# An attention and routing kernel on one core: a table-driven order of instructions in which small table pieces move behind a later GpSimd subtraction, and the first pair of heads runs in another order

## The chip, the cores and the metric

The kernel runs on one core of a Trainium2 chip. Five engines work side by side, each on its own list of instructions: PE (TensorE, matrix products), DVE (VectorE), ACT (ScalarE), POOL (GpSimd) and SP (SyncE, which here only issues transfers). An engine takes its list strictly in order; if the next instruction waits for another engine, everything behind it waits too. The metric is the time of one execution on the device, in microseconds (us). The kernel before was timed at 1265.13 us (median of 3 runs, 1263.82 to 1270.05). Its profile comes from one separate execution.

## What is computed

Attention over 64 heads with queries averaged in pairs of rows, then a mixture of experts with a greedy, capacity-limited assignment of tokens. Cut to what matters:

```python
# q, k, v: 8 x 8 x 1152 x 64 (q and k 8 times as wide as v)
q_pool = q.reshape(8, 8, 576, 2, 64).mean(axis=3)
scores = q_pool @ k.transpose(0, 1, 3, 2) / 8
scores = scores - scores.max(-1)
attn = exp(scores) / sum(exp(scores))
x = (attn @ v).transpose(0, 2, 1, 3).reshape(4608, 512)
logits = x @ w_gate                        # 4608 tokens x 8 experts
for idx in argsort(-logits.flatten()):     # greedy: best pair first,
    tok, e = idx // 8, idx % 8             # at most 576 tokens an expert
    if assigned[tok] < 0 and counts[e] < 576:
        assigned[tok] = e; counts[e] += 1
for e in range(8):
    out[assigned == e] = relu(x[assigned == e] @ w1[e]) @ w2[e]
```

## The kernel before, in words

The 64 heads are taken as 32 pairs. A pair needs 18 steps (two heads, nine blocks of 128 keys each). In a step (`step`, L734) PE forms scores of 128 keys against 576 queries (`sc`, L751), ACT takes their exponential into `P` (L754), and a remainder `PM` = `P` minus its leading half is formed by one subtraction of 128 x 576 elements (L758), on POOL in 16 of the 18 steps of a middle pair and on DVE in the other two. PE then uses `P` and `PM` as weights in the weighted sum of the values (`av`, L768).

Beside the steps of one pair the next pair is prepared. Queries and keys are split into a leading half and a remainder: `QH` and `KH` by ACT (L583, L601), `QL` and two halves of `KL` by DVE from two inputs (L591, L610). SP's transfers bring these into the layouts `QA`, `QB`, `KA`, `KB` and `BD`. The raw queries `QS` arrive by a transfer of SP, and POOL's queue issues a second one that adds the odd rows (L486). A bound on the scores of each query is needed: PE multiplies leading halves (`ma`, `mb`, L668), DVE takes maxima of them into `MX` (L671, L680), folds them into `CM` (L703), PE transposes it and DVE writes the bound row `AU` (L724), which goes into `QB`. Scores of the next pair can't start without it. Before the split, `bounds` finds the scales `SC` and the exponent's factor `EX` from sums of absolute values that ACT takes (L507).

The first pair differs. Its maxima run a head at a time (`max_chunk`, L649 to L662), in 15 pieces of 384 columns a head, for which the first head may use the banks of `sc` and `av` too, since nothing else uses them yet. Its remainders `QL` and `KL` and those of the second pair come from POOL.

Small constant tables for the routing (`routing_tables`) are made while attention runs: POOL makes index rows first, and then `pieces`, each one or two small instructions (`before` L326, `upto` L327, `e8`, `pcol`, four of `nib` with L331, `diag` L335 to L337, `slots` L340, `jval` L342, and two more), one a pair from the early pairs on. One piece, `same16` (L338, L339), is on DVE.

The order of instructions is written by a table of numbers. Every operation has a tag, a running number and the pair that it belongs to; its due time is the tag's number from `TAU` plus 25 for each pair (`TAU0`, `TAU1` and `TAU2` hold the first three pairs). `Cycle.plan` emits, among the operations whose inputs have been emitted, always the one with the lowest due time. So the tables alone say in which order each engine's list stands. The pieces have the tag `tab`, the piece on DVE `tad`. Operations of the second pair get their times of adding from `at` (L906).

Of the kernel before, what the change touches and what calls it, by code (L numbers as in the profile page):

```python
# [152 lines left out]
class Cycle(Order):  # L153
# [11 lines left out]
    def plan(self):  # L165
# [27 lines left out]
TAU = {"abs": [-48.4833, -47.0605, -38.3773], "aug": [-21.4881], "augd": [-11.2262, 4.4303], "augt": [-4.3451],  # L193
# [3 lines left out]
       -301.8994, -63.224, -198.6406, -15.9845, -78.5836, 33.7202, -197.7787], "bdd": [-52.3637, -285.2947], "best":  # L197
       [30], "el": [-77.0706], "ex": [-50.7557], "expa": [-16.6599, -154.184, -20.8529, 5.9927, 12.6026, 14.7889,
       -14.7359, -29.1238, -104.9479], "expb": [-32.523, -130.2187, -27.9823, 14.3985, 17.5253, -281.0359, 9.6164,
# [3 lines left out]
       [-70.8466, -187.4708], "ldq": [-65.2457], "ldv": [-277.9826], "ldw": [2.8], "me": [-19.8978, -10.7115,  # L203
# [6 lines left out]
       [2.7664, 4.9823, 6.5534, 8.0795, 9.6086, -181.5656, 16.9348, 19.0221, 21.216], "qkb": [5.2308, 7.0644, 8.3738,  # L210
       12.1143, 0.0557, 20.0132, 22.5039, 25.3261, 28.3165], "ql": [-38.1313], "rc": [9.2364, -9.47], "sc":
       [-36.4174], "scv": [-30.065], "spr": [-21.9235, -31.1405, -21.9627, -26.5265, -22.5479, -164.2155, -315.3032,
       -74.6622, -15.1485, -17.1123, -19.956, -16.4269], "store": [-95.7261], "sx": [16.3692, 22.2312, 0.8466,
       -61.2066, -78.1894], "tab": [-69.9737], "tad": [-127.8336], "tap": [-44.6145, -41.1498, -47.4908, -31.2065],
       "vh": [-26.7285, -47.8828], "vl": [-23.1603, -21.3115], "vs": [-148.6017, -208.4574], "vsh": [-168.3274],
       "wsq": [12.8365], "x": [-94.3595, -7.6786]}
TAU0 = {"abk": [-60.377, -62.9993], "abs": [-96.8953, -53.0217], "aug": [-7.39949, -0.804], "augt": [-7.399491,
# [5 lines left out]
        -7.026297, 1.533201, 4.734301, 9.325501, 23.883701], "expb": [-7.399487, -7.399467, -7.399445, -7.399424,  # L223
        1.198702, 3.416501, 5.503401, 22.1687, 22.168703], "fill": [-10.2794, -126.6764, -30.3842, -147.957,
        -245.9624, -174.4366, -139.2362, -212.3909, -147.5215, -160.7165, -141.2792, -181.6421], "fold": [-7.399497,
# [11 lines left out]
        1.5332, 4.7343, 9.3255, 23.8837], "qkb": [-7.399488, -7.399468, -7.399446, -7.399425, 1.198701, 3.4165,  # L237
        5.5034, 13.319, 22.168702], "ql": [-29.9917], "qs": [-147.1978], "rc": [9.181703, 25.133714], "sc":
        [-60.376997], "scv": [-37.467499], "spr": [-60.376977, -38.883998, -35.21, -60.37698, -31.0808, -29.991699,
# [6 lines left out]
TAU1 = {"abs": [-34.9327, -39.4214, -46.3877], "aug": [-1.025495], "augd": [-1.025494, -1.025493], "augt":  # L246
# [29 lines left out]
def routing_tables(nc, pool, ident, jp, scratch, do):  # L276
# [14 lines left out]
    it = {}  # L291
# [59 lines left out]
def attention(ctx, tc, top, kt, qt, v, wg, w1, x_dram, L, npair=NPAIR):  # L351
# [297 lines left out]
    def max_chunk(n, j, c, z, t):  # L649

        i = n % 2
        if n == 0:
            h, j = j // 5, j % 5
            banks = [(ma, "ma"), (mb, "mb")]
            if not h:
                banks += [(sc[a // 2][:, a % 2], ("sc", a // 2, a % 2)) for a in range(4)] + [(av[b], f"av{b}") for b in range(2)]
            m, mk = banks[z % len(banks)]
# [993 lines left out]
```

## Time and profile before

| | |
|---|---|
| timed runs, median of 3 | 1265.13 us (1263.82 to 1270.05) |
| the profiled execution, its time | 1275.09 us |
| its span, first to last instruction | 1273.3 us |
| PE busy | 1202.7 us, 94% |
| DVE busy | 1034.3 us, 81% |
| ACT busy | 974.6 us, 77% |
| POOL busy | 905.9 us, 71% |
| mean granted TensorE clock | 0.98 |

The span is what the profile's rows cover; the time of the profiled execution is 1.8 us more. Attention with everything beside it takes about the first 800 us, routing and the experts the rest. The busy shares are means over the whole span: which engine holds up which is read from the rows of a stretch.

### The profile page before, as it was taken

To read this page: it belongs to the slowest core of one execution; us is meant where nothing else is said; L and a number is where in the kernel's file an instruction comes from. 1 tells how busy PE (TensorE), PEld (TensorE's weight loads), DVE (VectorE), ACT (ScalarE), POOL (GpSimd) and SP (SyncE) were. 2 spreads that over 40 slices of the span, in tenths; PEclk is the share of its full clock that TensorE was granted. 3 is DMA by queue.
4 is the path that set the end of the run, shared out by engine and by line. 5 is a ranking of instruction groups with operands and counts; after the bars stand their busy time and mean duration, and the time that the engine had idled before them with its cause. 6 is when DMAs were issued, how large, how long until landed. Compare 5 with 4: busy or idle time off the path is not lost.

```text
span 1273.3 us, 38899 instructions
## 1 busy us (share of the span) xinstructions
PE 1202.7 (94%) x15470; PEld 865.0 (68%) x15470; DVE 1034.3 (81%) x2743; ACT 974.6 (77%) x1719; POOL 905.9 (71%) x879
## 2 busy tenths in 40 slices
PE   7899899898999999999999999789899899999998
PEld 2567677776777777877777778565657466565563
DVE  5889899898999999999999995788878788884520
ACT  6779789797899999999999986076765676767751
POOL 5779799697889988888898897055756474665641
PEclk7999999898999999999999999999999999999999
DMA  6676677566667768677776731043254454537401
GB/s 184 159 187 171 155 174 189 142 163 164 170 162 196 178 163 203 169 171 192 174 187 162 183 91 37 20 170 112 97 195 125 133 172 135 170 124 230 119 30 38
DMA packets 131218, 190.83 MB, mean 150 GB/s; under 512 B 50268, under 2 KB 86108, under 8 KB 128732
## 3 DMA queue, kind: packets, MB, share of 16 engines
q1 hardware_dynamic: 117948, 126.75, 37.9%
q0 software_dynamic: 12944, 61.58, 17.0%
q8 instruction: 121, 1.98, 0.7%
q14 instruction: 61, 0.50, 0.1%
q10 hardware_dynamic: 144, 0.02, 0.0%
HBM read 116.41 MB, written 18.87 MB: 106 GB/s over the span
## 4 chain that ended last, share of the span: by engine, by line
PE 69%; DVE 17%; ACT 4%; issue 3%; DMA 3%; SPq 1%; POOL 1%; another core or an unknown queue 1%; POOLq 0%; ACTq 0%; DVEq 0%
PE sc L751 19%; PE av L768 16%; PE ph L1536 9%; PE po L1566 8%; PE mb L668 5%; PE ma L668 4%; DVE MX L671 2%; DVE KL L610 1%; PE av L803 1%; DMA XG<-XB 1%; DVE PM L758 1%; DVE GE L1163 1%; DVE HX L1545 1%; DMA BD<-QH 1%; PE av L815 1%
## 5 line engine op out<-in xcount | busy, mean ns | idle before, releaser
L758 POOL TENSOR_TENSOR PM<-P 128x576 f16<-128x576 f32 x508 | 618.3, 1277 | 117.2 <-ACT P L754 65.2
L754 ACT ACTIVATE P<-sc,EX 128x576 f32<-128x576 f32 x576 | 412.7, 738 | 97.2 <-PE sc L751 84.2
L768 PEld LDWEIGHTS <-P 128*128 128x128 bf16 x5760 | 297.2, 98 | 31.3 <-issue 2.6
L768 PE MATMUL av<-V,P 128*128 128x65 f16 (+1 forms) x5760 | 305.3, 193 | 0.0
L768 PE MATMUL av<-V,PM 128*128 128x65 f16 x2880 | 296.4, 195 | 0.0
L768 PEld LDWEIGHTS <-PM 128*128 128x128 f16 x2880 | 265.7, 97 | 0.0
L751 PE MATMUL sc<-QA,KA 128*128 128x288 f16 x1152 | 236.7, 287 | 1.6 <-ACT P L754 1.3
L751 PE MATMUL sc<-QB,KB 65*128 65x288 f16 (+1 forms) x1152 | 237.9, 287 | 0.0
L671 DVE TENSOR_REDUCE MX<-mb 128x1 f32<-128x512 f32 x279 | 190.9, 684 | 32.3 <-PE mb L668 27.3
L671 DVE TENSOR_REDUCE MX<-ma 128x1 f32<-128x512 f32 x279 | 191.0, 685 | 13.3 <-PE ma L668 10.1
L751 PEld LDWEIGHTS <-KA 128*128 128x128 f16 x1152 | 106.9, 97 | 86.0 <-issue 34.9
L1566 PE MATMUL po<-W2H,HX 128*128 128x512 f16 x512 | 156.9, 381 | 0.3 <-ACT OT L1568 0.3
L1536 PE MATMUL ph<-XH,W1H 128*128 128x320 f16 (+1 forms) x512 | 146.3, 286 | 0.7 <-DVE WE L1514 0.3
L1536 PE MATMUL ph<-XL,W1H 128*128 128x320 f16 (+1 forms) x512 | 146.2, 286 | 0.8 <-DVE XL L1395 0.3
L1536 PE MATMUL ph<-XH,W1L 128*128 128x320 f16 (+1 forms) x512 | 145.9, 286 | 0.9 <-issue 0.9
L751 PEld LDWEIGHTS <-KB 65*128 65x128 f16 (+1 forms) x1152 | 113.3, 98 | 30.4
L1566 PEld LDWEIGHTS <-HX 128*128 128x128 f16 x768 | 71.6, 98 | 86.4 <-issue 9.6
L1588 POOL DMA_INDIRECT out_dram<-OT,idx x40 | 39.1, 979 | 118.9 <-ACT OT L1568 99.7
L668 PE MATMUL mb<-KH,BD 128*128 128x512 f16 x279 | 107.3, 384 | 13.6 <-DVE AU L724 11.3
L1536 PEld LDWEIGHTS <-W1H 128*128 128x128 f16 x1024 | 97.5, 98 | 33.2 <-issue 7.7
L668 PE MATMUL ma<-KH,BD 128*128 128x512 f16 x279 | 106.8, 383 | 5.9 <-DMA BD<-QH 2.4
L1489 POOL TENSOR_TENSOR W2L<-W,W2H 128x512 f16<-128x512 f32 x64 | 73.3, 1158 | 40.8 <-ACT W L1487 33.6
(308 smaller groups left out, 2169.7 us busy)
## 6 DMA issues: line engine op xcount, KB each, us to landing
KD<-in_kt_dram SPq DMA_DIRECT2D x64, 288.0 KB
VD<-in_v_dram SPq DMA_DIRECT2D x32, 576.0 KB
WB<-in_w_dram SPq DMA_DIRECT2D x32, 512.0 KB
QA<-QH SPq DMA_DIRECT2D x128, 72.0 KB
KA<-KH SPq DMA_DIRECT2D x64, 144.0 KB
KA<-KL SPq DMA_DIRECT2D x64, 144.0 KB
KB<-KH SPq DMA_DIRECT2D x64, 144.0 KB
x_dram<-X SPq DMA_DIRECT2D x16, 576.0 KB
```

The lines of the kernel that those rows point to most:

```text
L610: fn=lambda h=h: nc.vector.scalar_tensor_tensor(KL[n % 2][:, h], KD[n % 2][:, h], KS, KH[i][:, h], op0=OP.mult, op1=OP.subtract),
L668: od.add(t, "PE", 214, lambda: nc.tensor.matmul(m, BD[i][:, j, :], KH[i][:, 512 * c:512 * c + 512], start=True, stop=True), r=bd + [("KH", ...
L671: od.add(t, "DVE", 597, lambda: nc.vector.tensor_reduce(MX[i][:, j, c:c + 1], m, axis=AX.X, op=OP.max), r=[mk], w=[("MX", i, j, c)], tag=" ...
L751: nc.tensor.matmul(c[:, t, :288], a[i][:rows, s, ks], b[i][:rows, s, 288 * t:288 * t + 288], start=first, stop=not first)
L754: od.add(g + 0.1, "ACT", 624, lambda: nc.scalar.activation(p.rearrange("p (t q) -> p t q", t=2), c[:, :, :288], AF.Exp, scale=EX[n % 3][:, ...
L758: od.add(g + 0.2, en, dur, lock=1, fn=lambda: eng.tensor_tensor(pm, p, hi, op=OP.subtract), r=[("P32", g % NP)], w=[("PM", g % NM)], tag="pm")
L768: nc.tensor.matmul(out, w[:, qs], v, start=kb == 0 and j == 0 and y == 0, stop=kb == NKB - 1 and y == 2, skip_group_check=True)
L803: nc.tensor.transpose(m[:, 128 * z:128 * z + 128], X[u][:, 3 * q + z], ident)
L1489: od.add(tt, "POOL", 1230, lambda o=lo[p], a=raw[p], h=hi[p]: nc.gpsimd.tensor_tensor(o, a, h, op=OP.subtract), r=[key, hk, sk], w=[(nm + ...
L1536: nc.tensor.matmul(p, a[:, d, fs], b[:, d, qs], start=z == 0, stop=z == 11)
L1566: nc.tensor.matmul(o, a[:, z, q0:q0 + 128], b[:, z], start=z == 0 and y == 0, stop=z == 7 and y == 2)
L1588: st = nc.gpsimd.indirect_dma_start(out=out, out_offset=bass.IndirectOffsetOnAxis(ap=idx[i][:n, c:c + 1], axis=0), in_=OT[ob][:n], in_offs ...
```

## The change

It has two parts, and both alter orders and hardly any operations.

In the steady run, the due time of the tag `tab` goes from -69.97 to -60.4, and the DVE piece is cut into two pieces of one instruction each.

In the first pair and the beginning of the second, new numbers in `TAU0`, `TAU1` and `at` give: five banks instead of eight for the first head's maxima and two in turn for the second's; the first head's bound row directly behind its fold; the first exponentials ahead of ACT's sums of absolute values for the second pair; and one clearing of `KB` on POOL in another place. The numbers of `TAU2`, and those of `TAU` other than `tab`, are the same.

```diff
-       ... "tab": [-69.9737], ...
+       ... "tab": [-60.4], ...
...
-TAU1 = {"abs": [-34.9327, -39.4214, -46.3877], ...
+TAU1 = {"abs": [-32.3994884, -32.3994916, -46.3877], ...
...
-        (1000, lambda: (nc.vector.tensor_scalar(it["m"], it["m"], 15, None, op0=OP.bitwise_and),
-                       nc.vector.tensor_scalar(C["same16"], it["m"], 0.0, None, op0=OP.is_equal))),
+        (1000, lambda: nc.vector.tensor_scalar(it["m"], it["m"], 15, None, op0=OP.bitwise_and)),
+        (1000, lambda: nc.vector.tensor_scalar(C["same16"], it["m"], 0.0, None, op0=OP.is_equal)),
...
-            banks = [(ma, "ma"), (mb, "mb")]
-            if not h:
-                banks += [(sc[a // 2][:, a % 2], ("sc", a // 2, a % 2)) for a in range(4)] + [(av[b], f"av{b}") for b in range(2)]
-            m, mk = banks[z % len(banks)]
+            if h:
+                m, mk = ((ma, "ma"), (mb, "mb"))[z % 2]
+            else:
+                m, mk = ((ma, "ma"), (av[0], "av0"), (sc[0][:, 0], ("sc", 0, 0)), (av[1], "av1"), (sc[1][:, 0], ("sc", 1, 0)))[(5 * c + j) % 5]
...
-                at.update(load=-61.5, vload=-57, split=-42.5, bound=-42, spread=-34, val=-36, mm=-20, fold1=1, aug=1.5)
+                at.update(load=-61.5, vload=-57, split=-31.6, bound=-31.15, spread=-23.5, val=-29, mm=-20, fold1=1, aug=1.5)
```

The lists below show the orders that follow. A row names the line, the operation, and its tiles as out<-in with buffer numbers. Lines of the kernel after stand five higher (L758 is L763 there, L591 is L596, L327 is L332).

POOL's list around the piece `upto` and the transfer of `QS0` that follows it, before:

```order
L758 TENSOR_TENSOR PM3_153<-P323_143 128x576
L758 TENSOR_TENSOR PM6_156<-P326_146 128x576
L327 TENSOR_SCALAR upto_176<-jp_70 128x128
L758 TENSOR_TENSOR PM5_155<-P325_145 128x576
L758 TENSOR_TENSOR PM7_157<-P327_147 128x576
L758 TENSOR_TENSOR PM0_150<-P320_140 128x576
L758 TENSOR_TENSOR PM9_159<-P329_149 128x576
L758 TENSOR_TENSOR PM2_152<-P322_142 128x576
L758 TENSOR_TENSOR PM1_151<-P321_141 128x576
L758 TENSOR_TENSOR PM3_153<-P323_143 128x576
L486 DMA QS0_124<-in_qt_dram 128x576
```

And the same stretch of POOL's list after:

```order
L763 TENSOR_TENSOR PM3_153<-P323_143 128x576
L763 TENSOR_TENSOR PM6_156<-P326_146 128x576
L763 TENSOR_TENSOR PM5_155<-P325_145 128x576
L763 TENSOR_TENSOR PM7_157<-P327_147 128x576
L763 TENSOR_TENSOR PM0_150<-P320_140 128x576
L763 TENSOR_TENSOR PM9_159<-P329_149 128x576
L763 TENSOR_TENSOR PM2_152<-P322_142 128x576
L763 TENSOR_TENSOR PM1_151<-P321_141 128x576
L332 TENSOR_SCALAR upto_176<-jp_70 128x128
L763 TENSOR_TENSOR PM3_153<-P323_143 128x576
L491 DMA QS0_124<-in_qt_dram 128x576
```

The piece moved from the fourth place of the stretch to the place just ahead of the last subtraction before the transfer. The other pieces move to the same place, each between the same two transfers of `QS` as before.

DVE's list where the `same16` piece stands before, among the maxima of a pair (`MX1`):

```order
L671 TENSOR_REDUCE MX1_139<-mb_171 128x1
L338 TENSOR_SCALAR scratch_112<-scratch_112 128x128
L339 TENSOR_SCALAR same16_182<-scratch_112 128x128
L680 TENSOR_REDUCE MX1_139<-ma_170 128x4
L671 TENSOR_REDUCE MX1_139<-mb_171 128x1
L671 TENSOR_REDUCE MX1_139<-ma_170 128x1
L671 TENSOR_REDUCE MX1_139<-mb_171 128x1
```

And where it stands after, later in the same pair:

```order
L685 TENSOR_REDUCE MX1_139<-mb_171 128x4
L676 TENSOR_REDUCE MX1_139<-ma_170 128x1
L343 TENSOR_SCALAR scratch_112<-scratch_112 128x128
L344 TENSOR_SCALAR same16_182<-scratch_112 128x128
L596 SCALAR_TENSOR_TENSOR QL0_91<-QS0_124,SC2_115,QH0_89 128x576
L615 SCALAR_TENSOR_TENSOR KL0_87<-KD0_119,SC2_115,KH0_85 128x576
L763 TENSOR_TENSOR PM8_158<-P328_148 128x576
```

The two instructions moved from the middle of the pair's maxima to the place just ahead of `QL` and `KL`.

ACT's list around the first exponentials of the program (`P321`, `P320`, `P323`, `P322`), before:

```order
L507 ACTIVATE VJ_134,VQ_128<-VD1_123 128x1152
L507 ACTIVATE VJ_134,VM1_127<-QS1_125 128x576
L507 ACTIVATE VJ_134,VM1_127<-KD1_120 128x1152
L754 ACTIVATE P321_141<-sc1_167,EX0_116 128x576
L539 ACTIVATE SC1_114<-VE1_136 128x2
L547 ACTIVATE EX1_117<-SC1_114 128x1
L548 ACTIVATE EX1_117<-VE1_136 128x1
L583 ACTIVATE QH1_90<-QS1_125,SC1_114 128x576
L754 ACTIVATE P320_140<-sc0_166,EX0_116 128x576
L754 ACTIVATE P323_143<-sc1_167,EX0_116 128x576
L601 ACTIVATE KH1_86<-KD1_120,SC1_114 128x576
```

And after:

```order
L512 ACTIVATE VJ_134,VQ_128<-VD1_123 128x1152
L759 ACTIVATE P321_141<-sc1_167,EX0_116 128x576
L512 ACTIVATE VJ_134,VM1_127<-QS1_125 128x576
L759 ACTIVATE P320_140<-sc0_166,EX0_116 128x576
L512 ACTIVATE VJ_134,VM1_127<-KD1_120 128x1152
L759 ACTIVATE P323_143<-sc1_167,EX0_116 128x576
L544 ACTIVATE SC1_114<-VE1_136 128x2
L552 ACTIVATE EX1_117<-SC1_114 128x1
L553 ACTIVATE EX1_117<-VE1_136 128x1
L759 ACTIVATE P322_142<-sc0_166,EX0_116 128x576
L588 ACTIVATE QH1_90<-QS1_125,SC1_114 128x576
```

Three exponentials of the first head now stand ahead of or between the sums L507 (now L512), and `SC1`, `EX1` and `QH1` of the second pair stand behind them. SP's list is the same before and after, so its transfers that need `QH1` stay ahead of those that bring the second head's keys.

## Rows read from the trace of the kernel before

**Rows 1.** Stretches: window, length, PE, PEld, DVE, ACT, POOL busy (count), clock, DMA, GB/s.

```profile
120.00:330.00 210.00, 198.75 (x3203) 156.56 (x3202) 190.10 (x351) 177.17 (x308) 169.19 (x156) 0.96 0.64 160
440.00:780.00 340.00, 338.61 (x5659) 268.93 (x5656) 306.66 (x608) 305.36 (x525) 293.93 (x252) 1.00 0.67 165
```

**Rows 2.** Timeline at 126 us, DVE: start, us, engine, line, operation, tiles, count.

```profile
126.34 0.80 DVE L591 SCALAR_TENSOR_TENSOR QL<-QS,SC,QH 128x576 f16<-128x576 f32 x1
...
127.79 1.70 DVE L758 TENSOR_TENSOR PM<-P 128x576 f16<-128x576 f32 x1
130.43 3.29 DVE L610 SCALAR_TENSOR_TENSOR KL<-KD,SC,KH 128x576 f16<-128x576 f32 x1
```

**Rows 3.** Timeline at 126 us, ACT, POOL and PE; in brackets the idle time before.

```profile
126.24 1.36 ACT L754 ACTIVATE P<-sc,EX 128x576 f32<-128x576 f32 x2
...
127.73 1.15 POOL L758 TENSOR_TENSOR PM<-P 128x576 f16<-128x576 f32 x1 [1.51 <-issue]
...
129.47 3.62 POOL L758 TENSOR_TENSOR PM<-P 128x576 f16<-128x576 f32 x3
...
134.90 0.38 PE L668 MATMUL mb<-KH,BD 128*128 128x512 f16 x1 [3.35 <-DVE AU L724]
```

**Rows 4.** Timeline at 697 us, the same place of a later pair: DVE, ACT, POOL.

```profile
697.73 0.81 DVE L591 SCALAR_TENSOR_TENSOR QL<-QS,SC,QH 128x576 f16<-128x576 f32 x1
...
698.21 1.36 ACT L754 ACTIVATE P<-sc,EX 128x576 f32<-128x576 f32 x2
...
699.18 0.75 DVE L758 TENSOR_TENSOR PM<-P 128x576 f16<-128x576 f32 x1
...
699.70 1.24 POOL L758 TENSOR_TENSOR PM<-P 128x576 f16<-128x576 f32 x1 [2.09 <-issue]
```

**Rows 5.** Timeline at 223 and 422 us, the same place of two other pairs, and 302 us.

```profile
223.65 1.36 ACT L754 ACTIVATE P<-sc,EX 128x576 f32<-128x576 f32 x2
223.70 0.80 DVE L591 SCALAR_TENSOR_TENSOR QL<-QS,SC,QH 128x576 f16<-128x576 f32 x1
...
302.49 4.59 DVE L610 SCALAR_TENSOR_TENSOR KL<-KD,SC,KH 128x576 f16<-128x576 f32 x1 [0.25 <-issue]
...
422.15 1.36 ACT L754 ACTIVATE P<-sc,EX 128x576 f32<-128x576 f32 x2
422.16 0.80 DVE L591 SCALAR_TENSOR_TENSOR QL<-QS,SC,QH 128x576 f16<-128x576 f32 x1
```

**Rows 6.** Timeline, DVE's `QL` of four more pairs.

```profile
177.50 0.80 DVE L591 SCALAR_TENSOR_TENSOR QL<-QS,SC,QH 128x576 f16<-128x576 f32 x1
...
276.40 0.81 DVE L591 SCALAR_TENSOR_TENSOR QL<-QS,SC,QH 128x576 f16<-128x576 f32 x1
...
444.78 0.80 DVE L591 SCALAR_TENSOR_TENSOR QL<-QS,SC,QH 128x576 f16<-128x576 f32 x1
...
743.65 0.80 DVE L591 SCALAR_TENSOR_TENSOR QL<-QS,SC,QH 128x576 f16<-128x576 f32 x1
```

**Rows 7.** Timeline, POOL's table pieces `upto`, one of `nib`, and `diag`.

```profile
118.52 0.54 POOL L327 TENSOR_SCALAR upto<-jp 128x128 bf16<-128x128 int32 x1
...
216.03 0.25 POOL L331 TENSOR_SCALAR nib<-scratch 128x16 f32<-128x16 int32 x1
...
320.04 0.37 POOL L335 TENSOR_SCALAR scratch<-scratch 128x64 f32<-128x64 int32 x1
320.48 0.38 POOL L336 TENSOR_SCALAR diag<-scratch 128x64 f16<-128x64 int32 x1
```

**Rows 8.** Timeline at 343 us, PE behind the DVE pieces.

```profile
343.35 0.38 PE L668 MATMUL ma<-KH,BD 128*128 128x512 f16 x1 [1.08 <-DVE MX L680]
```

**Rows 9.** Timeline, first pair: ACT and SP's queue.

```profile
26.79 0.74 ACT L754 ACTIVATE P<-sc,EX 128x576 f32<-128x576 f32 x1 [3.32 <-PE sc L751]
28.04 0.76 ACT L583 ACTIVATE QH<-QS,SC 128x576 f16<-128x576 f32 x1
...
37.78 0.60 SPq L617 DMA_DIRECT2D KB<-KH  x1
```

More of the change, by code (lines that the diff above doesn't have):

```diff
@@ L192 @@
 PERIOD = 25.0
-TAU = {"abs": [-48.4833, -47.0605, -38.3773], "aug": [-21.4881], "augd": [-11.2262, 4.4303], "augt": [-4.3451],
[3 rows of a table removed]
-       -301.8994, -63.224, -198.6406, -15.9845, -78.5836, 33.7202, -197.7787], "bdd": [-52.3637, -285.2947], "best":
-       [30], "el": [-77.0706], "ex": [-50.7557], "expa": [-16.6599, -154.184, -20.8529, 5.9927, 12.6026, 14.7889,
-       -14.7359, -29.1238, -104.9479], "expb": [-32.523, -130.2187, -27.9823, 14.3985, 17.5253, -281.0359, 9.6164,
[3 rows of a table removed]
-       [-70.8466, -187.4708], "ldq": [-65.2457], "ldv": [-277.9826], "ldw": [2.8], "me": [-19.8978, -10.7115,
[6 rows of a table removed]
[L210 to L216, printed above, removed]
@@ L217 @@
-TAU0 = {"abk": [-60.377, -62.9993], "abs": [-96.8953, -53.0217], "aug": [-7.39949, -0.804], "augt": [-7.399491,
[5 rows of a table removed]
-        -7.026297, 1.533201, 4.734301, 9.325501, 23.883701], "expb": [-7.399487, -7.399467, -7.399445, -7.399424,
-        1.198702, 3.416501, 5.503401, 22.1687, 22.168703], "fill": [-10.2794, -126.6764, -30.3842, -147.957,
-        -245.9624, -174.4366, -139.2362, -212.3909, -147.5215, -160.7165, -141.2792, -181.6421], "fold": [-7.399497,
[11 rows of a table removed]
-        1.5332, 4.7343, 9.3255, 23.8837], "qkb": [-7.399488, -7.399468, -7.399446, -7.399425, 1.198701, 3.4165,
-        5.5034, 13.319, 22.168702], "ql": [-29.9917], "qs": [-147.1978], "rc": [9.181703, 25.133714], "sc":
-        [-60.376997], "scv": [-37.467499], "spr": [-60.376977, -38.883998, -35.21, -60.37698, -31.0808, -29.991699,
[6 rows of a table removed]
@@ L246 @@
-TAU1 = {"abs": [-34.9327, -39.4214, -46.3877], "aug": [-1.025495], "augd": [-1.025494, -1.025493], "augt":
[6 rows of a table removed]
-        -16.355199, -23.751799, -15.081299, -21.213299, -10.492399, -18.345799, -13.433399, -1.025498], "mre":
-        [-27.9644, -1.0255, -8.404399], "qa": [-68.5572], "qh": [-32.399481], "ql": [-28.143899], "sc": [-32.399483],
-        "scv": [-24.0828], "spr": [-32.39945, -9.0591, -32.399452, -32.399477, -17.2565, -9.3805, -32.399451, -1.8944,
-        -32.399453, -32.399478, -32.399476, -5.7004], "vd": [1.4358, 1.435801], "vh": [-24.082798, -24.082799], "vl":
-        [1.435803, 1.435802], "vs": [-32.399489, -32.399485], "vsh": [-32.399484]}
@@ L258 @@
-TAU2 = {"abs": [-44.485199, -38.0633, -27.5185], "aug": [-0.158697], "augd": [-0.158696, -0.158695], "augt":
[10 rows of a table removed]
+TAU = {"abs": [-48.4833, -47.0605, -38.3773], "aug": [-21.4881], "augd": [-11.2262, 4.4303], "augt":
[4 rows of a table added]
+       -197.7787], "bdd": [-52.3637, -285.2947], "best": [30], "el": [-77.0706], "ex": [-50.7557], "expa":
+       [-16.6599, -154.184, -20.8529, 5.9927, 12.6026, 14.7889, -14.7359, -29.1238, -104.9479], "expb":
+       [-32.523, -130.2187, -27.9823, 14.3985, 17.5253, -281.0359, 9.6164, -75.1771, -33.9254], "fold":
[3 rows of a table added]
+       -187.4708], "ldq": [-65.2457], "ldv": [-277.9826], "ldw": [2.8], "me": [-19.8978, -10.7115, -7.4221],
[3 rows of a table added]
+       -148.0081, -65.768, -132.0348, -32.0039, -97.7545, -264.0034, -48.0572, -20.7891], "mre": [-214.7953,
[3 rows of a table added]
+       16.9348, 19.0221, 21.216], "qkb": [5.2308, 7.0644, 8.3738, 12.1143, 0.0557, 20.0132, 22.5039, 25.3261,
+       28.3165], "ql": [-38.1313], "rc": [9.2364, -9.47], "sc": [-36.4174], "scv": [-30.065], "spr":
+       [-21.9235, -31.1405, -21.9627, -26.5265, -22.5479, -164.2155, -315.3032, -74.6622, -15.1485, -17.1123,
+       -19.956, -16.4269], "store": [-95.7261], "sx": [16.3692, 22.2312, 0.8466, -61.2066, -78.1894], "tab":
+       [-60.4], "tad": [-127.8336], "tap": [-44.6145, -41.1498, -47.4908, -31.2065], "vh": [-26.7285,
+       -47.8828], "vl": [-23.1603, -21.3115], "vs": [-148.6017, -208.4574], "vsh": [-168.3274], "wsq":
+       [12.8365], "x": [-94.3595, -7.6786]}
@@ new lines @@
+TAU0 = {"abk": [-60.377, -62.9993], "abs": [-96.8953, -53.0217], "aug": [-7.3994978, -7.399479], "augt":
[5 rows of a table added]
+       -7.3994829, -7.3994788, -7.0263, -7.026297, 1.533201, 4.734301, 9.325501, 23.883701], "expb":
+       [-7.3994936, -7.3994862, -7.39948, -7.399424, 1.198702, 3.416501, 5.503401, 22.1687, 22.168703],
+       "fill": [-10.2794, -126.6764, -160.7165, -147.957, -245.9624, -174.4366, -139.2362, -212.3909,
+       -147.5215, -28.0, -141.2792, -181.6421], "fold": [-7.3994986, -7.3994794], "kd": [-38.884, -60.376976,
+       -48.9739], "kh": [-60.376993, -60.376988], "kl": [-38.883999, -60.376975], "ld": [-238.2482, -167.2286,
+       -196.0025], "ldv": [-155.2937], "ldw": [-22.91], "mm0": [-60.3, -60.29, -60.28, -60.298, -60.288,
[9 rows of a table added]
+       1.5332, 4.7343, 9.3255, 23.8837], "qkb": [-7.3994944, -7.3994914, -7.3994846, -7.399425, 1.198701,
+       3.4165, 5.5034, 13.319, 22.168702], "ql": [-29.9917], "qs": [-147.1978], "rc": [9.181703, 25.133714],
+       "sc": [-60.376997], "scv": [-37.467499], "spr": [-60.376977, -38.883998, -35.21, -60.37698, -31.0808,
+       -29.991699, -19.3372, -5.7954, 1.1987, -5.2047, -29.4859, -23.4536], "vd": [-25.831599, -25.831598],
+       "vh": [-25.8316, -37.467498], "vl": [-25.831597, -24.1066], "vs": [-60.376999, -60.376998, -53.021699,
+       -53.021698], "vsh": [-53.0], "wsq": [8.3999], "wu": [-94.0011, -63.9847, -63.984699, -63.984698,
+       -63.984697, -63.984696, -63.984695, -63.984694, -63.984693, -61.9197], "wx": [-29.6554009, -7.3994998,
+       -7.3994996, -7.3994994, -7.3994992, -7.3994966, -7.3994964, -7.3994962, -7.399496, -7.3994918,
+       -7.3994896, -7.3994868, -7.3994836], "x": [16.5429, 25.133715]}
@@ new lines @@
+TAU1 = {"abs": [-32.3994884, -32.3994916, -46.3877], "aug": [-1.025495], "augd": [-1.025494, -1.025493],
+       "augt": [-1.025496], "bdd": [-32.39948, -32.399479], "el": [-32.3994834], "ex": [-32.3994832], "fold":
[11 rows of a table added]
+TAU2 = {"abs": [-44.485199, -38.0633, -27.5185], "aug": [-0.158697], "augd": [-0.158696, -0.158695], "augt":
[8 rows of a table added]
+       [-26.02549], "scv": [-26.025488], "spr": [-24.599189, -20.382799, -23.4618, -13.2415, -10.3208,
+       -26.02548, -24.599199, -20.382798, -24.599197, 1.8542, 1.9169, -21.7404], "vh": [-23.1713, -26.025479],
+       "vl": [-16.7131, -26.025478], "vs": [-26.025492, -26.025491], "vsh": [-26.025489]}
```

96 rows, old and new, of tables (TAU, TAU0, TAU1, TAU2) are left out of this document.

## The prediction, made before the changed kernel ran

> **What bounds the kernel now.** I read the stretches first. From 440 to 780 us PE is busy 338.61 of 340 us at a granted clock of 1.00; from 120 to 330 us it is busy 198.75 of 210 at 0.96 [rows 1]. So the late pairs are bound by PE, and an order of other engines can give them nothing. The early pairs, in which the table pieces stand, lose time to something. The second view was PE's waits, which led to the timelines. In the pair at 126 us DVE's second half of `KL` takes 3.29 us [rows 2], while POOL runs three subtractions without a break from 129.47 to 133.09 [rows 3]; the row of `KL` ends at 133.72. The bound row `AU` is behind it in DVE's list, and PE stands idle 3.35 us for `AU` [rows 3]. In the same place of the pair at 697 us the like DVE instruction, `QL`, takes 0.81 us [rows 4]. I call such an event a lock-out: a DVE operation with two inputs doesn't get on while POOL's subtractions follow each other.
>
> What decides is a race. At 126 us DVE starts `QL` at 126.34 and reaches its first subtraction `PM` at 127.79, but POOL began its last subtraction at 127.73, 0.06 us earlier, and that `PM` takes 1.70 us [rows 2, 3]. At 697 us DVE's `PM` starts at 699.18, half a microsecond ahead of POOL's at 699.70, and takes 0.75 us [rows 4]. POOL's last subtraction waits for the second of two exponentials, so I measure the race by the start of these exponentials minus the start of `QL`: -0.10 at 126 us (lost), +0.48 at 697 us (won). Two closer cases fix the edge: -0.05 at 223 us and -0.01 at 422 us [rows 5]. The first was lost, as its pitch shows (below), the second won, as its pitch to the next pair shows, 444.78 - 422.16 = 22.62 us [rows 5, 6]. So DVE wins when the difference is above about -0.03.
>
> The price of a lock-out comes from the pitch. Thirteen undisturbed pairs give (743.65 - 444.78) / 13 = 22.99 us [rows 6]. From 126.34 to 177.50 are two pairs, 51.16 us: 5.2 more than 45.98 [rows 2, 6]. From 223.70 to 276.40 are 52.70: 6.7 more [rows 5, 6]. The mean is 6.0. A third, the 4.59 us `KL` at 302.49 [rows 5], begins late in its pair, where the race is with POOL's transfer of `QS`; nothing in the change touches it, and I leave it in both sums.
>
> **The change, part by part.**
>
> The table pieces on POOL. Their old place is within the run of six subtractions that ends ahead of `QL`'s; each pushes the run back by its length, and DVE's own subtraction in front of `QL`. That is how the margin of +0.48 was eaten. In the new place the piece stands between the sixth and the last subtraction, where POOL waits 1.51 us at 126 us and 2.09 us at 697 us [rows 3, 4]. That idle time hides a piece on POOL itself: `upto` takes 0.54 us, a `nib` instruction 0.25, the two instructions of `diag` together 0.82, from 320.04 to 320.86 [rows 7]. So the pairs at 126 and 223 us get their margin back, before the new cost: -5.2 and -6.7, together -11.9 us.
>
> The new cost is that the piece runs right when DVE asks for `QL`. At 126 us the gap on POOL starts at 127.73 - 1.51 = 126.22, 0.12 us ahead of `QL` [rows 2, 3]. If POOL's piece holds `QL` off as POOL's subtraction holds off `PM`, `QL` starts later by the piece's length less 0.12, and the difference of the race is 0.48 - (length - 0.12) = 0.60 - length. For `upto` that gives +0.06, won by about 0.09; for a `nib` piece with its small clearing, some 0.35 in all by my estimate, +0.25, won; for `diag` -0.22, lost. No row shows a piece directly ahead of `QL`, so the bounds are: no delay at all (nothing lost, 0 us) and, above, all pieces of about 0.45 us or more losing, four of them (`before`, `upto`, `diag`, and the two instructions of `slot1` and `jval`), 4 x 6.0 = 24 us. I take one loss, `diag`, +6.0, since the rows at -0.05 and -0.01 [rows 5] are nearest to its -0.22.
>
> On this point the Trainium skill, page "SBUF — State Buffer", section "Who interferes with whom", says that a DVE instruction with two inputs in SBUF contends with a GpSimd instruction that reads SBUF, though not with one that only writes it, and that whichever was issued first keeps the other out until it is done. The 1.70 us `PM` and the 3.29 us `KL` agree with it. It speaks against the new place, since every piece but the clearing in `nib` reads; by it, `nib` would count with 0.25 us alone and the sum stays as it is.
>
> The DVE piece. In its old place in the middle of the maxima it makes PE wait 1.08 us for a bank [rows 8]. In its new place ahead of `QL` it stands where PE has no bank to wait for that soon; -1.1 us. It then delays `QL` itself, in a pair whose POOL piece is short; the margin of 0.48 covers part of it. Bounds: -1.1 and, if that pair falls into a lock-out, +6.0 - 1.1 = +4.9. I take -1.1.
>
> The first pair. The first exponential starts at 26.79 after ACT has waited 3.32 us [rows 9]. With the bound row directly behind the fold, and the transpose not behind other maxima, I estimate the start some 3 us earlier, bounded by that wait of 3.32. Against it, the sums for the second pair no longer lie in this idle time, and three more exponentials of 0.74 us stand ahead of `QH1`, 2.2 us: `QH1`, before at 28.04, comes by my estimate 2 us later [rows 9]. SP's list is unchanged, and the second head's keys are issued at 37.78 [rows 9], behind transfers that wait for `QH1`; they come about 2 us later too. So the second head's scores, though their bound row is ready sooner, start at about the same time, and what the first head gains in front is waited away in its middle. Bounds: -3.3 (the wait is gone and nothing gives it back) and +2.2 (the whole delay is on the path). I take +0.5, nearer to the middle.
>
> The sum on the profiled execution: 1275.09 - 11.9 + 6.0 - 1.1 + 0.5 = 1268.6 us, 6.5 less. That execution lies 10.0 us above the median of the timed runs, which themselves spread over 6.2 us, about the price of one lock-out; so the timed runs may hold fewer lock-outs than the profile, and the gain could be smaller there. I apply the difference to the median: 1265.13 - 6.5 = 1258.6, and round it to 1259.5 for that doubt.
>
> **The rivals.**
>
> None new. `diag` doesn't hold `QL` off, since its two instructions leave a gap of 0.07 us between them (320.41 to 320.48 [rows 7]) into which `QL` may slip. Then 1265.13 - 12.5 = 1252.6. Against it: the subtractions on POOL at 129.47 also follow one another, and `KL` didn't slip in there until the run ended [rows 2, 3].
>
> As many as before. `diag` loses and so does `upto`, whose margin above the edge is only 0.09 us, or the pair with the DVE piece. Two new for two old: -11.9 + 12.0 - 1.1 + 0.5 = -0.5, 1264.6. The smallness of that margin speaks for it; against it is that the edge lies where DVE already won with -0.01.
>
> Slower. One mechanism, the piece in front of `QL`, decides more pairs than it saves: if the real margin of the early pairs is smaller than the +0.48 of the late ones by 0.15 us or more, pieces above 0.45 us lose, which are four. -11.9 + 24.0 - 1.1 + 0.5 = +11.5, 1276.6; with three it is +5.5, 1270.6. It decides from the third loss on. For it: the early pairs run at a clock of 0.96 in the mean and are less settled [rows 1]. Against it: at 126 us the margin is 0.58 smaller than at 697, and the 0.54 of `upto` in its old place explains that [rows 2 to 4, 7]. This is also what the rule of the Trainium skill named above ("SBUF — State Buffer", "Who interferes with whom") comes to if every reading piece is issued ahead of `QL`; the traces show it for subtractions only.
>
> **How the numbers follow.** Chances: one new lock-out 0.37, none 0.20, as many as before 0.25, three or more 0.18. The likeliest is 1259.5, with 1255 to 1264 as its own range from the prologue's bounds. The range 1251 to 1271 leaves out the worse half of the slower case and the end of the best one. About 0.5%, 6.3 us, is what a measurement here can tell from no change. Below 1258.8 lie the case of none new and a bit over half of the likeliest: 0.40. Above 1271.5 lies the slower case: 0.18 as rounded with what the prologue may add to the third. The rest, 0.42, is within.
>
> **What would show it.** In the profile after, at the pairs of 126 and 223 us, `QL` should start ahead of the exponentials, `KL` take under 1 us and `AU` not be waited for. In the pair of `diag`, near 320 us, `QL` should start 0.7 us behind the sixth subtraction, DVE's `PM` take over 1.5 us, a `KL` over 3 us, and PE wait some 3 us for `AU`. PE's 1.08 us wait behind the DVE piece should be gone. In the first pair the first exponential should start near 23.7 us and `QH1` near 30. The prediction is wrong if `QL` starts on time although a piece runs, if pieces of half a microsecond lose, or if the second head's first scores move by more than 2 us.

## The result, and the profile after

The changed kernel took 1249.69 us (median of 4 runs, 1246.4 to 1251.49) against 1264.47 us before (4 runs, 1256.53 to 1270.05): a ratio of 0.9892, with a 95% interval of 0.9848 to 0.9936, 14.8 us less. The forecast was 1259.5 us with a range of 1251 to 1271, so the time lies 1.3 us below the range. The direction was right, the size was not. The rival "none new" (1252.6) came nearest.

The stretches of the profile after, in the columns of [rows 1]:

```profile
120.00:330.00 210.00, 206.41 (x3402) 163.40 (x3400) 192.48 (x373) 188.53 (x327) 180.66 (x167) 0.98 0.69 173
440.00:780.00 340.00, 337.95 (x5673) 269.37 (x5672) 303.59 (x597) 302.33 (x516) 293.81 (x253) 1.00 0.64 159
```

From 120 to 330 us PE is now busy 206.41 us where it was 198.75 [rows 1]; the late pairs are as they were. The pair of `upto`, on DVE, POOL and ACT (it answers to [rows 2, 3], with lines five higher):

```profile
128.05 0.80 DVE L596 SCALAR_TENSOR_TENSOR QL<-QS,SC,QH 128x576 f16<-128x576 f32 x1
...
129.51 0.74 DVE L763 TENSOR_TENSOR PM<-P 128x576 f16<-128x576 f32 x1
131.18 0.81 DVE L615 SCALAR_TENSOR_TENSOR KL<-KD,SC,KH 128x576 f16<-128x576 f32 x1
...
127.91 0.54 POOL L332 TENSOR_SCALAR upto<-jp 128x128 bf16<-128x128 int32 x1
129.99 1.27 POOL L763 TENSOR_TENSOR PM<-P 128x576 f16<-128x576 f32 x1 [1.54 <-issue]
...
128.49 1.36 ACT L759 ACTIVATE P<-sc,EX 128x576 f32<-128x576 f32 x2
```

`QL` starts 0.44 us ahead of the exponentials and DVE's `PM` 0.48 ahead of POOL's subtraction: the race is won, and `KL` takes 0.81 us instead of 3.29. `upto` begins 0.14 us ahead of `QL`, as forecast, but `QL` takes 0.80 us all the same: nothing holds it. The pair of `diag`, for which a new lock-out was forecast:

```profile
317.13 0.81 DVE L596 SCALAR_TENSOR_TENSOR QL<-QS,SC,QH 128x576 f16<-128x576 f32 x1
...
318.59 0.75 DVE L763 TENSOR_TENSOR PM<-P 128x576 f16<-128x576 f32 x1
...
317.00 0.37 POOL L340 TENSOR_SCALAR scratch<-scratch 128x64 f32<-128x64 int32 x1
317.43 0.75 POOL L341 TENSOR_SCALAR diag<-scratch 128x64 f16<-128x64 int32 x1
319.11 1.24 POOL L763 TENSOR_TENSOR PM<-P 128x576 f16<-128x576 f32 x1 [0.93 <-POOL diag L341]
```

Here too `QL` isn't held. It is the piece that waits: L341 takes 0.75 us instead of 0.38 [rows 7], since `QL` began before it. One lock-out is left, the one that was left out of the sum:

```profile
291.43 4.59 DVE L615 SCALAR_TENSOR_TENSOR KL<-KD,SC,KH 128x576 f16<-128x576 f32 x1 [0.25 <-issue]
...
291.12 0.89 POOL L491 DMA_DIRECT2D QS<-in_qt_dram  x1
291.75 3.65 POOL L763 TENSOR_TENSOR PM<-P 128x576 f16<-128x576 f32 x3
...
297.20 0.58 PE L673 MATMUL mb<-KH,BD 128*128 128x512 f16 x1 [3.28 <-DVE AU L729]
```

After an idle time of 0.25 us this `KL` starts 0.31 us behind POOL's issue of the transfer of `QS`, and it ends behind the three subtractions that follow. In the pair of `upto` the like `KL` starts at 131.18, 0.02 us ahead of the issue at 131.20, and isn't held. The next rows tell of the first pair (the first exponential, `QH1`, the second head's first exponential, SP's issue of its keys) and of the last `QL`:

```profile
22.90 0.74 ACT L759 ACTIVATE P<-sc,EX 128x576 f32<-128x576 f32 x1 [2.46 <-PE sc L756]
29.69 0.76 ACT L588 ACTIVATE QH<-QS,SC 128x576 f16<-128x576 f32 x1
...
44.17 1.51 ACT L759 ACTIVATE P<-sc,EX 128x576 f32<-128x576 f32 x2 [2.30 <-PE sc L756]
...
39.50 0.59 SPq L622 DMA_DIRECT2D KB<-KH  x1
...
730.69 0.80 DVE L596 SCALAR_TENSOR_TENSOR QL<-QS,SC,QH 128x576 f16<-128x576 f32 x1
```

The last `QL` stands at 730.69, before at 743.65 [rows 6]: 13.0 us less up to there. The rest of the span is 1247.2 - 730.69 = 516.5 us, where it was 1273.3 - 743.65 = 529.65: 13.1 us less behind all that the change touches. That last part is read below; it turns out not to be a gain of the change.

### The profile page after: what moved, and what is told of

Same layout as the page of the kernel before. It is cut to its first block, busy times and chain, and to the rows that moved or that the text cites. A ratio compares the mean times of both kernels' runs of the same rounds, so it can differ in the third digit from the quotient of the medians.

```text
span 1247.2 us, 38894 instructions
## 1 busy us (share of the span) xinstructions
PE 1196.7 (96%) x15470; PEld 864.8 (69%) x15470; DVE 1022.5 (82%) x2743; ACT 972.7 (78%) x1719; POOL 901.2 (72%) x879
## 4 chain that ended last, share of the span: by engine, by line
PE 75%; DVE 11%; DMA 6%; ACT 3%; issue 3%; SPq 1%; POOL 1%; POOLq 0%; ACTq 0%; DVEq 0%
PE sc L756 21%; PE av L773 18%; PE ph L1541 11%; PE po L1571 10%; PE mb L673 5%; PE ma L673 5%; DMA W<-in_w_dram,widx 2%; DVE MX L676 1%; PE av L808 1%; DMA BD<-QH 1%; ACT P L759 1%; PE av L820 1%; PE rt L1174 1%; DVE HX L1550 1%; DVE GE L1168 1%
## 5 line engine op out<-in xcount | busy, mean ns | idle before, releaser
L763 POOL TENSOR_TENSOR PM<-P 128x576 f16<-128x576 f32 x508 | 612.9, 1265 | 107.6 <-ACT P L759 57.1
```

Of the source, the lines that this page charges most:

```text
L763: od.add(g + 0.2, en, dur, lock=1, fn=lambda: eng.tensor_tensor(pm, p, hi, op=OP.subtract), r=[("P32", g % NP)], w=[("PM", g % NM)], tag="pm")
```

## The experiments

Three theories stood at the start. A: the gain is the lock-outs that the old place of the pieces caused, and the first pair costs a little. B: the gain comes from the first pair or from the routing stage. On the lock-out that is left: F, it comes from the place in DVE's list, or G, from that pair's data and transfers. Kernels of one group ran on one chip; the chips differ (before: 1262.3, 1259.9, 1285.6 and 1278.8 us), so times are compared within a group or by their ratio to before. Each experiment has one profile, of one execution.

**The kernel before, profiled again** (no edit).

> The kernel before, unchanged, profiled once more. If the lock-outs are fixed by the order, KL takes 3.29 us near 130 and 227 us and 4.59 us near 302 us again, and the time from the last QL to the end may differ from the 529.65 us of the first profile. If they are chance, one or more of them is gone or stands elsewhere. If the 13.1 us that the profile after is shorter behind the last QL belong to the change, that stretch is within 2 us of 529.65; if they are chance of the routing stage, it lies some 5 to 13 us lower here, with the same order.

1270.87 us. DVE's long `KL`, in the columns of [rows 2], and below them what PE waited for behind the attention (us in total, times, longest), of this execution and of the first:

```profile
108.24 3.32 DVE L610 SCALAR_TENSOR_TENSOR KL<-KD,SC,KH 128x576 f16<-128x576 f32 x1
...
136.05 3.29 DVE L610 SCALAR_TENSOR_TENSOR KL<-KD,SC,KH 128x576 f16<-128x576 f32 x1
...
234.63 3.28 DVE L610 SCALAR_TENSOR_TENSOR KL<-KD,SC,KH 128x576 f16<-128x576 f32 x1
...
307.65 4.59 DVE L610 SCALAR_TENSOR_TENSOR KL<-KD,SC,KH 128x576 f16<-128x576 f32 x1 [0.25 <-issue]
...
337.20 3.29 DVE L610 SCALAR_TENSOR_TENSOR KL<-KD,SC,KH 128x576 f16<-128x576 f32 x1
...
754.10 0.81 DVE L591 SCALAR_TENSOR_TENSOR QL<-QS,SC,QH 128x576 f16<-128x576 f32 x1
```

```profile
PE rt L1179 <- DVE red L1175: 3.6, 10, 0.8
```

```profile
PE rt L1179 <- DVE red L1175: 14.6, 15, 2.9
```

With the same order there are four lock-outs of the race where the first profile had two (the pairs at 103 and 328 us joined those at 126 and 223), and the one at 302 us again. So the number varies, and a sum made on one profile can miss by 12 us. Over all experiments, the three profiles with the pieces in the old place have 2, 4 and 2 lock-outs of the race; the eleven with the pieces in the new place, without a ladder and without the earlier `KH` (both below), have none.

Behind the last `QL` this execution needs 1269.1 - 754.10 = 515.0 us, about as the changed kernel, with the same order as in the first profile. Of the difference of 14.65 us to the first profile, 11.0 are PE waiting for `red`. The other profiles show what this stretch goes by. In the two groups in which before was timed at 1262.3 and 1259.9 us, all eight profiles need 513.2 to 519.2 us here and wait 3.2 to 4.0 us for `red`; in the two groups with before at 1285.6 and 1278.8 us, all seven need 532.9 to 540.2 us and wait 11.1 to 13.7 us. The steady part alone was profiled in a group of each kind:

```profile
PE rt L1179 <- DVE red L1175: 3.2, 10, 0.6
```

```profile
PE rt L1179 <- DVE red L1175: 13.5, 12, 3.0
```

So this stretch goes by the group and not by the order, and it makes up most of the 16 to 26 us by which the times of before differ between the two kinds. The first profile is near the slower kind and the profile after is of the faster one: the 13.1 us are no gain of the change. What sets a group's kind no run shows.

**The due time of `tab` alone; the first pair alone; the steady part alone** (`tab` and the cut of the DVE piece, without the first pair).

```diff
-       ... "tab": [-69.9737], ...
+       ... "tab": [-60.4], ...
```

> The kernel before with the due time of the tag tab at -60.4 and nothing else of the change. Theory A (the pieces in their old place ate the margin of the race, in the new place they don't hold QL off): no lock-out near 126 and 223 us, none in the pair of diag, the one near 300 us stays; QL of the last pair 12 to 15 us earlier than the 743.65 of before, time 12 to 15 us less. Theory B (the gain comes from the first pair or from the routing stage): less than 6 us.

> The kernel before with the new first pair alone. Theory A: QL of the third pair moves from 56.36 to about 58.2, the lock-outs near 128, 229 and 304 us stay; time 1 to 3 us more than before. Theory B (the first pair brings a part of the gain, or its shift moves the race): time 3 us less or more, or a lock-out gone.

> The change without its first pair: the due time of tab and the cut of the DVE piece. Theory A: as the kernel after from the third pair on, with QL of the third pair at 56.4 as before; 12 to 17 us less than before, about 1.8 less than the kernel after. Theory B: slower than the kernel after.

On one chip, before at 1262.27: `tab` alone 1243.84 us, 0.9859 (0.982 to 0.9898), 18.4 less; the first pair alone 1258.79, 0.9978 (0.9951 to 1.0006), not told from no change; the steady part alone 1241.83, 0.9847 (0.9807 to 0.9887). The one number gives the gain, more than the 12 to 15 us that theory A had, and theory B falls. For the first pair alone theory A had 1 to 3 us more; its median is 3.5 us lower, within the noise. In `tab` alone and in the steady part no race is lost; the lock-out near 290 us is there in both. The same `KL` as in [rows 2] and the last `QL`, with `tab` alone:

```profile
130.63 0.81 DVE L610 SCALAR_TENSOR_TENSOR KL<-KD,SC,KH 128x576 f16<-128x576 f32 x1
...
729.99 0.80 DVE L591 SCALAR_TENSOR_TENSOR QL<-QS,SC,QH 128x576 f16<-128x576 f32 x1
```

That `QL` stands 13.7 us ahead of the first profile of before, which has two lock-outs more, and 24.1 ahead of the second, which has four more: 6.8 and 6.0 us each, with the gain from the DVE piece in it. The first pair alone keeps its lock-outs:

```profile
108.82 3.32 DVE L612 SCALAR_TENSOR_TENSOR KL<-KD,SC,KH 128x576 f16<-128x576 f32 x1
...
228.87 3.28 DVE L612 SCALAR_TENSOR_TENSOR KL<-KD,SC,KH 128x576 f16<-128x576 f32 x1
```

`tab` alone also moved the DVE piece to its new place: all pieces write one chain named `tables`, so the DVE piece can't be emitted before `diag`. Its cut into two did nothing for that.

**A ladder of copies, a ladder of multiplications.** Ahead of each piece on POOL stands one instruction more that reads w elements of each partition and writes as many, w rising from 130 to 1040.

```diff
+            G.tensor_copy(dump[:, :w], scratch[:, :w])       # or
+            G.tensor_scalar(dump[:, :w], scratch[:, :w], 1.0, None, op0=OP.mult)
+            fn()
...
```

> The steady part alone, with a copy of 128 x w from int32 to float16 ahead of each table piece on POOL, w rising from 130 to 1040 (one result tile more, read by nobody). Theory A (a reading piece holds QL off until it ends): QL takes longer in every pair from the first on, by the copy's length less 0.12 to 0.4 us, and from a piece of about 0.7 us on the pair loses its race, KL 3 us. Theory C (short reading pieces don't hold QL off, only long ones do, as slots with 0.71 us did by 0.36): QL at 0.81 us up to w of about 520, longer above; lost from about 0.9 us of copy on.

> As the ladder of copies, with a multiplication by 1 of the same sizes in place of the copy. If only the length of the reading piece decides, QL's length rises from the same piece length as with copies (0.5 to 0.6 us: 0.84 to 0.95 there) and a pair is lost from about 1 us of piece ahead of QL on. If the form decides, QL stays at 0.81 with multiplications up to 1 us, as it did beside upto (0.54 us).

1254.41 us with copies, 1285.31 with multiplications, on different chips. The rows of w = 390 and 1040 (with multiplications 130 too), each instruction of POOL above the `QL` that it meets, first with copies:

```profile
214.75 0.51 POOL L351 CAST dump<-scratch 128x390 f16<-128x390 int32 x1
...
214.92 0.95 DVE L604 SCALAR_TENSOR_TENSOR QL<-QS,SC,QH 128x576 f16<-128x576 f32 x1
...
462.78 1.05 POOL L351 CAST dump<-scratch 128x1040 f16<-128x1040 int32 x1
...
462.94 1.50 DVE L604 SCALAR_TENSOR_TENSOR QL<-QS,SC,QH 128x576 f16<-128x576 f32 x1
```

And with multiplications:

```profile
129.25 0.54 POOL L351 TENSOR_SCALAR dump<-scratch 128x130 f16<-128x130 int32 x1
129.39 0.80 DVE L604 SCALAR_TENSOR_TENSOR QL<-QS,SC,QH 128x576 f16<-128x576 f32 x1
...
220.74 1.19 POOL L351 TENSOR_SCALAR dump<-scratch 128x390 f16<-128x390 int32 x1
220.88 0.98 DVE L604 SCALAR_TENSOR_TENSOR QL<-QS,SC,QH 128x576 f16<-128x576 f32 x1
...
473.80 2.85 POOL L351 TENSOR_SCALAR dump<-scratch 128x1040 f16<-128x1040 int32 x1
473.94 1.52 DVE L604 SCALAR_TENSOR_TENSOR QL<-QS,SC,QH 128x576 f16<-128x576 f32 x1
```

Theory A fails, since pieces of 130 elements leave `QL` at 0.80 us; theory C has the direction, but sets in too late, since `QL` grows from 390 elements on and not from 520. At w = 390 a copy of 0.51 us and a multiplication of 1.19 us stretch `QL` by about the same, 0.15 and 0.18; at 1040 a copy of 1.05 and a multiplication of 2.85 by 0.70 and 0.72. A multiplication of 0.54 us with 130 elements doesn't stretch it at all. So neither the length nor the form decides, and the expectation by length (from 0.5 us on) fails for the multiplications: the number of elements does. They are read and written alike here, so the runs don't tell which of the two counts. The copies' slope is (0.70 - 0.15) / 650 = 0.85 ns an element, and the `QL` of 1.07, 1.28 and 1.38 us at w = 520, 780 and 910 lie on this line within 0.02 us; for a piece that starts some 0.15 us ahead, the stretch begins by it at about 390 - 150 / 0.85, some 210 elements (an estimate from these rows). `slots` in the changed kernel, 640 elements, fits: 0.15 us + 250 x 0.85 ns = 0.36 us, and its `QL` takes 1.16 us:

```profile
409.30 1.16 DVE L596 SCALAR_TENSOR_TENSOR QL<-QS,SC,QH 128x576 f16<-128x576 f32 x1
...
409.13 0.71 POOL L345 CAST slots<-scratch 128x640 f16<-128x640 int32 x1
```

Two pairs of each ladder were lost all the same. With copies `KL` takes 3.27 us at 340.54 (w = 780) and 415.29 (w = 910); with multiplications `QL` takes 4.83 us at 345.44 and the remainder of the values 5.38 us at 429.66. At w = 1040 no race was lost, so the stretch alone doesn't decide; what lost these four stays open.

**The changed kernel again, DVE's list shifted, `KH` earlier.** The shift puts 20 more clearings on DVE in the idle time ahead of the first queries; the third kernel changes one due time, the first number of `kh`, from -31.3132 to -32.8. Both start from the steady part alone.

```diff
+            for _ in range(20):
+                nc.vector.memset(PM[-1][:, :64], 0.0)
```

> The changed kernel once more, for a comparison with the version that has its steady part alone. Theory A (the new first pair costs 1.8 us, since QH of the second pair and with it the second head's keys come later): 1.5 to 4 us above the version without the new first pair, which was at 0.9847 of before. Theory B (the new first pair gains or does nothing): at or below 0.9847.

> The steady part alone, with 20 small clearings more on DVE in the idle time at 3 to 5.5 us, so that every later DVE instruction stands 20 places further in its list. Theory F (the last lock-out, 4.59 us of KL in the pair near 282 us, comes from the fetch of DVE's list, since that KL is the one instruction that starts 0.3 us late behind nothing, about 500 places into the list): the 4.59 us are gone and the time is some 6 us less. Theory G (it belongs to the data or the transfers of that pair): KL takes 4.59 us there again, time as without the clearings.

> The steady part alone, with the second half of KH one exponential earlier on ACT (kh -32.8), so that the second KL of a pair stands right behind PM on DVE and far ahead of POOL's transfer. If the tie of that KL with the transfer is all that makes the last lock-out, it is gone: some 6 us less than the steady part alone. If the exponential that is put back, or the maxima behind KL, come too late, POOL's last subtraction or AU is late in many pairs: 10 us more or worse.

The changed kernel repeated its ratio, 0.9892 (0.9857 to 0.9927; 1246.97 against 1259.87 us). With the shift the `KL` of the last lock-out takes 0.82 us and no lock-out is left. Its time, 1246.59 (0.9869), isn't below the steady part's ratio. In its profile the clearings run 3.1 us and the third pair's `QL` stands at 65.13, where the steady part has 54.68, with PE granted 0.50 of its clock (1.2 GHz) from 10 to 40 us; whether that ate the gain in the timed runs too isn't shown. With `KH` earlier the time was 1322.88 us, 1.0483 (1.0429 to 1.0536): a miss, and an instructive one. `KL` no longer meets POOL's run, but another two-input instruction does, in every second pair:

```profile
132.58 5.86 DVE L645 SCALAR_TENSOR_TENSOR V<-VD,SC,V 128x576 f16<-128x576 f32 x1
```

POOL's run behind the transfer of `QS` now has eight subtractions without a break, from 128.71 to 137.82 us. The remainder of the values begins in its midst and ends 0.62 us behind it, 5.86 us for an operation of 0.81. A lock-out that is avoided for one operation was handed to the next in the list.

**The second head's transfers moved; the clearings moved to POOL.** In the first, from the changed kernel, the last eight of the twelve `spr` numbers of `TAU0` are lowered to just below -33, so that the second head's keys and queries leave ahead of `QH` of the second pair. In the second, from the steady part alone, the ten clearings of `PM` stand on POOL:

```diff
-            for x in (P32, PM):
-                for i, y in enumerate(x):
-                    nc.vector.memset(y[:, M:] if i < NKB else y[:, :64], 0.0)
+            for i, y in enumerate(P32):
+                nc.vector.memset(y[:, M:] if i < NKB else y[:, :64], 0.0)
...
+            for i, y in enumerate(PM):
+                nc.gpsimd.memset(y[:, M:] if i < NKB else y[:, :64], 0.0)
```

> The changed kernel with the transfers that lay out the second head of the first pair moved ahead of those of QH of the second pair in SP's list. Theory A (with the new first pair the second head waits in its middle only because its transfers stand behind QH in SP's list): its first scores start near 38 us where the changed kernel has 42.9, and QL of the third pair comes 2 to 5 us earlier than 58.2; time 2 to 5 us less than the changed kernel (ratio 0.985 to 0.988). Theory B (the second pair's own chain sets the end of this stretch): QL of the third pair stays at 58 or comes later, since BD and KH of the second pair now leave some 2 us later.

> The steady part alone, with the ten clearings of PM taken from DVE to POOL, into POOL's idle time at 23 to 27 us, so that every later DVE instruction stands ten places nearer the front of its list and nothing else moves. Theory F (fetch of DVE's list): the 4.59 us of KL near 282 us are gone, QL of the third pair at 54 to 57 us, QL of the last pair about 6 us earlier than 724.9; time 5 to 7 us less than the steady part alone, near 0.980 of before. Theory G: KL takes 4.59 us in that pair again.

The first gave 1272.94 us, 0.9908 (0.9875 to 0.9941), no better than the changed kernel and not the 0.985 to 0.988 that theory A had. Its second head's scores waited for no transfer any more, but the third pair's `QL` stands at 63.41 where the changed kernel has 58.18. PE was granted 0.50 of its clock (1.2 GHz) from 20 to 40 us, where the profile of the changed kernel has 0.85; what the transfers are worth stays open:

```profile
20.00:40.00 20.00, 16.13 (x52) 5.27 (x53) 9.05 (x22) 10.87 (x20) 8.03 (x8) 0.50 0.42 112
```

The second gave 1268.66, 0.9885 (0.9833 to 0.9937), above the 0.980 that was expected, on a chip on which the steady part alone was not timed; no lock-out was left in its profile.

**Four kernels on one chip**: the changed kernel and the steady part alone, each with and without the clearings moved.

> The changed kernel, on one chip with the three below. Theory A: as the first time, 0.987 to 0.992 of before, and 0.3 to 0.5% above the steady part alone, since its first pair costs 2 to 4 us. Theory B (the first pair is worth nothing either way): equal to the steady part alone within 0.2%.

> The steady part alone, again. Theory A: 0.983 to 0.987 of before.

> The changed kernel with the ten clearings of PM on POOL. Theory F (place in DVE's list): no lock-out near 290 us, 5 to 7 us less than the changed kernel (0.4 to 0.55%).

> The steady part alone with the ten clearings of PM on POOL. Theory F: 5 to 7 us less than the steady part alone, the fastest of the four, near 0.980 of before. Theory G: as the steady part alone.

| | clearings on DVE | clearings on POOL |
|---|---|---|
| changed kernel | 1265.53 us, 0.9891 (0.9843 to 0.9938) | 1259.82 us, 0.9854 (0.9804 to 0.9905) |
| steady part alone | 1263.20 us, 0.9876 (0.9828 to 0.9925) | 1260.18 us, 0.9853 (0.9801 to 0.9904) |

The second `KL` of the pair near 284 us, the steady part without and with the clearings moved:

```profile
286.96 4.59 DVE L610 SCALAR_TENSOR_TENSOR KL<-KD,SC,KH 128x576 f16<-128x576 f32 x1 [0.25 <-issue]
```

```profile
290.81 0.82 DVE L613 SCALAR_TENSOR_TENSOR KL<-KD,SC,KH 128x576 f16<-128x576 f32 x1
```

Moving ten clearings out of DVE's list removes the last lock-out, as adding twenty did: it hangs on the place in the list, and theory G falls. In all twelve profiles that have this lock-out, its `KL` is the 521st instruction of DVE that the profile counts. That the fetch of the list makes it late is argued, not shown; with `KH` earlier, where another instruction has that place, DVE has no such idle time there. By the medians the removal is worth 5.7 and 3.0 us, where 5 to 7 were expected, and the single times of the kernels overlap. The first pair costs 2.3 us without the clearings moved and gives 0.4 with them: not told from zero. Both kernels with the clearings on POOL are faster than before, and their medians lie 5.7 and 5.4 us below the changed kernel's.

## Why the prediction missed

What held. The pieces in their old place ate the margin, and the lock-outs at 126 and 223 us were theirs: [rows 2, 3, 5] against the rows after, and one number gave it back alone. Per lock-out about 6 us was right (6.0 and 6.8 by `tab` alone). PE's 1.08 us wait behind the DVE piece [rows 8] is gone; from 330 to 352 us the profile after shows no wait of PE for DVE. The chain in the first pair ran as worked out: the first exponential earlier by 3.9 us (26.79 to 22.90), `QH1` later by 1.65 (28.04 to 29.69), the second head's keys later by 1.72 (37.78 to 39.50) [rows 9], and the second head's first scores later by 1.24 (41.67 to 42.91).

The step that failed is "if POOL's piece holds `QL` off as POOL's subtraction holds off `PM`, `QL` starts later by the piece's length less 0.12". It gave `diag` a new lock-out, +6.0. Measured: 0. `diag`'s first instruction reads 64 elements, `upto` 128, both under the 210 of the ladders, and only `slots` stretched `QL`, by 0.36 us, which cost no race. In eight other profiles with the pieces in the new place (the earlier `KH` left out) the `QL` near 103 us takes 1.26 or 1.27 us beside a subtraction of POOL that began ahead of it, and that pair isn't lost there either. I had priced a piece by the length of its row, and by the ladders the row of a small POOL instruction says little of how long it keeps DVE out. That is 6.0 of the 9.8 us between forecast and result.

Here the Trainium skill, page "SBUF — State Buffer", section "Who interferes with whom", has it that whoever issues first keeps the other out for the whole instruction. For POOL's piece as the first the runs differ: a multiplication of 2.85 us stretched the `QL` begun 0.14 us behind it by 0.72, and that `QL` ended at 475.46, 1.19 us ahead of the multiplication's end at 476.65. For `QL` as the first the trace agrees: L341, begun 0.30 us behind it, ended 0.24 us behind its end.

The second miss is the basis. The sum took the race's lock-outs of one profile, two; the next profile of the same kernel had four. `tab` alone took 18.4 us off on its chip, the whole change 14.8, both more than two lock-outs with 12. How many the timed runs of before hold no run shows; that they hold more than two fits these times. I saw that the timed runs spread over one lock-out's price and that the profile lay 10.0 us above their median, and concluded that the timed runs hold fewer. But that excess is no more than what the first profile spent behind the last `QL` beyond the faster groups, 529.65 us against 513.2 to 519.2, where I had not looked. So the 0.9 us that I added to the forecast for that doubt had no ground, and by the result the wrong sign.

The term of the first pair was mis-sized: +0.5 forecast. In the profile the third pair's `QL` moved from 56.36 to 58.18 us, +1.8, near the bound of +2.2; by the times of the four kernels it lies between -0.4 and +2.3 and can't be told from zero. The profiles speak for a cost up to that place: with the new first pair, in the order of the change, that `QL` stands at 56.8 to 59.0 us (five profiles), with the old one at 54.4 to 56.5 in nine of eleven, and beyond 61 in the two whose clock was 0.50 from 20 to 40 us.

The rivals "slower" and "as many as before" fell with the step that failed. "None new" was the right case, and 12.5 us its right sum for the first profile; its chance of 0.20 was too low, because I read rows of the subtraction (576 elements, two inputs) as rows of the piece (64 to 128 elements, one input).

## What to carry to other kernels

Where two engines shut each other out, look for a race of a tenth of a microsecond that is lost in some executions, and profile twice: the number of losses, not the one profile, is the price. Before a difference of two profiles is called a gain, compare the stretch that the change doesn't touch: here it differed by 13 us, and by the group of runs, not by the kernel. A small instruction may stand right ahead of the operation it could block if it has few elements (here up to some 210 in each partition); count elements, not the length of its row. And place a filler where its engine waits anyway, not within the run that sets the next start.

## What was unexpected of the hardware

A POOL instruction with one input that began some 0.15 us ahead held DVE's two-input operation by 0.85 ns for each element of a partition beyond some 210, whether its row was 0.51 or 1.19 us long at 390 elements. One lock-out stood at the same instruction of DVE's list in twelve profiles (4.59 or 4.60 us), in every kernel in which the number of instructions in front of it was kept, and was gone in the four in which the list was ten instructions shorter or twenty longer at the front. And the start of the program isn't steady: from 20 to 40 us the granted clock was 0.50 (1.2 GHz throughout) in one profile of the ladder of multiplications and 1.00 (2.4 GHz) in that of the copies, which have the same first pair, and the third pair's `QL` stood at 61.3 and 55.3 us.
